# Weight sums on GpSimd one step ahead of their rounding, all in the plain blocks, and attention visits placed by half steps

## Chip, cores and metric

The kernel runs on one core of a Trainium2 chip. The metric is the device time of one execution in microseconds (us). The engines are named as the profile names them: PE (matrix multiply), PEld (its weight loads), DVE (VectorE), ACT (ScalarE), POOL (GpSimd) and SP (SyncE, which here only issues DMAs). Each engine works through its own queue in order; an instruction whose inputs or buffers are not ready holds up everything behind it on that engine.

## What is computed

Local attention over chunks of 64 positions, whose output is the input of a two-layer network with a leaky activation (cut from the reference):

```python
scores = scale * np.matmul(q_c, k_c.transpose(0, 1, 2, 4, 3))   # chunks of 64
scores = scores - np.max(scores, axis=-1, keepdims=True)
attn = np.exp(scores)
attn = attn / (np.sum(attn, axis=-1, keepdims=True) + 1e-09)
out = np.matmul(attn, v_c)                                       # 8 x 8 x 576 x 64
x = out.transpose(0, 2, 1, 3).reshape(4608, 512)
h = x @ w_in                                                     # 512 x 2048
g = np.maximum(h, 0.0) + alpha * np.minimum(h, 0.0)
return g @ w_out                                                 # 2048 x 512
```

## The kernel before

Every float32 product is built from rounded pieces: a value is split into a high part (a rounded copy, by ACT) and a low part (the rest, by DVE), and a product takes three passes on PE.

The 4608 tokens are 36 attention tiles of 128, or nine token blocks of 512. The first three blocks (`PLAIN = 3`) are multiplied plainly, in 48 **steps**; a step is one block with one of 16 slices `f` of the hidden width: `ffn_in` (L318, 12 matmuls into `ps_h`), the activation `prelu` (L308 and L309 on ACT, L310 on DVE), a split (L330 on ACT gives `gh`, L331 on DVE gives `gl`), and `ffn_out` (L343, 12 matmuls into the four accumulators `ps_o0` to `ps_o3`). From step 20 on, the order on PE is kept as written, and the `ffn_out` of a step comes two `ffn_in` later, so the activation has about one step of slack. The steps run over block 0 (3 steps), block 1 (9), block 0 (13), block 1 (7) and block 2 (16). Where a run of steps ends, `store` copies the four accumulators to SBUF (L372, ACT): the first two go into the two halves of one staging buffer named `more`, the others into `ob` and a `g`. The next run of steps cannot write an accumulator before it has been copied.

The other six blocks are taken in three **pairs**, by a scheme with seven instead of eight products of half-size matrices. It needs seven combinations of the quarters of each weight pair. These are made during the plain steps and written to DRAM (`wi_a`, `wo_a`), from where they are streamed back in units of 512 KB. `combine` makes the four combinations that are sums, for one `(side, j)` of 16 (`wi` and `wo`, `j` 0 to 7): it adds high and low parts of two weight tiles back together (L498, two 128x512 adds into buffers `t1`, of which there are two), forms the sums (L505 to L508, four 128x256), rounds them (L519 on ACT, L520 on DVE) into a buffer `raw` (two of them) or `more` (one), and issues four DMAs to DRAM from POOL's queue (L476). `raw` and `more` were the landing buffers of the weights earlier on. A rounding therefore waits until the earlier content of its buffer has been written out, and so does the copy of an accumulator into `more`. The table `COMBINE` names the 14 steps at which a `combine` is emitted; the last two `wo` ones (`LATER`) are made inside the first pair.

`stream` (L540) issues the loads of the combined weights, also on POOL's queue: unit after unit into a ring of four buffers: the two `raw`, and the rooms `wi15` and `wo15` of the last slice's weights, which are free only after the last plain step has used them.

Attention goes on beside all this. For 14 tiles of the plain stage, and for more in the pairs, a **visit** does on PE the value product of an old tile (L279) and the scores of a new one (L201), then the softmax (L217, L218 on DVE, L221 on ACT, L223 to L225 on DVE), a transpose (L232, DVE) and eight small DMAs (L239, SP). The list `visits` names the steps before whose `ffn_in` a visit is placed.

Only PE's order is pinned from step 20 on. The order on the other engines is set by a scheduler that plays the program through in a model of time: what stands late in its model stands late in the queue.

## Time and profile before

| | us |
|---|---|
| median of 3 runs | 849.5 |
| lowest, highest | 849.36, 853.39 |
| the profiled execution | 855.14 |
| its span in the profile | 853.4 |
| PE busy / DVE / ACT / POOL | 810.4 / 672.0 / 544.9 / 208.4 |

The profile is of one execution, which took 5.6 us longer than the median of the others. Its parts used below are: the windows (busy time of each engine in a stretch, then PE's granted clock, the DMA engines' share and GB/s), the waits (who waited for whom: total, times, longest), the timeline (start, duration, engine, line, operation, operands, count, and in brackets the idle time ahead of it with what ended it), the groups by line (count | busy us, mean ns | idle before) and the DMA issues (count, KB each, median us from issue to landing). On this time axis step 20 begins near 158 us, the last plain step's `ffn_out` ends at 349 us, and the first pair's first weight product begins at 350.2 us.

### The profile page before, as it was taken

How to read it: one execution, taken by the hardware profiler on the slowest of the kernel's cores; microseconds unless marked ns; L12 is line 12 of the kernel's file. 1: busy time of each engine (PE TensorE's matmuls, PEld its weight loads, DVE VectorE, ACT ScalarE, POOL GpSimd, SP SyncE). 2: the span in 40 equal slices, each digit the busy share in tenths (PEclk: the TensorE clock that was granted, in tenths of full speed). 3: DMA queues.
4: the chain of work that ended last, by engine and by line, in shares of the span. 5: the costliest groups of instructions: out<-in, count | busy, mean ns of one | idle time of the engine just before them, and what ended most of it. 6: DMA issues, size and time to landing. Idle time of an engine off the chain costs nothing.

```text
span 853.4 us, 15390 instructions
## 1 busy us (share of the span) xinstructions
PE 810.4 (95%) x5248; PEld 645.8 (76%) x5248; DVE 672.0 (79%) x1267; ACT 544.9 (64%) x1392; POOL 208.4 (24%) x331
## 2 busy tenths in 40 slices
PE   4699999999699999999989999999999999999998
PEld 4567788777578778777767878777788778888886
DVE  5788999987978967587869997676689966658875
ACT  5976575656666766677776564777765536556552
POOL 3005223224442230111111233111122321111232
PEclk9899999999899999999999999999999999999999
DMA  9728778548767675679774789776567995555778
GB/s 259 223 72 293 258 234 277 199 150 219 244 173 208 220 247 162 222 255 299 253 259 161 234 230 322 264 246 236 165 203 236 237 310 191 191 180 195 233 222 236
DMA packets 76478, 192.40 MB, mean 225 GB/s; under 512 B 11888, under 2 KB 21104, under 8 KB 76272
## 3 DMA queue, kind: packets, MB, share of 16 engines
q0 software_dynamic: 37600, 125.32, 46.1%
q1 hardware_dynamic: 30656, 51.53, 19.2%
q10 hardware_dynamic: 8144, 14.56, 5.6%
q8 instruction: 42, 0.69, 0.3%
q14 instruction: 36, 0.29, 0.1%
HBM read 135.27 MB, written 42.99 MB: 209 GB/s over the span
## 4 chain that ended last, share of the span: by engine, by line
PE 61%; DMA 13%; DVE 10%; ACT 9%; SPq 4%; issue 2%; POOL 1%; DVEq 0%; ACTq 0%; POOLq 0%
PE ps_o L725 14%; PE ps_h L725 12%; PE ps_o L609 11%; PE ps_o L343 8%; PE ps_h L318 8%; PE ps_h L609 5%; SPq L239 4%; ACT pr L221 3%; DMA pT<-t 3%; DMA v_sb<-v 2%; DMA raw<-w_in 1%; DMA partial<-g 1%; DVE t L232 1%; DMA k_sb<-kT 1%; DMA wi<-qT 1%
## 5 line engine op out<-in xcount | busy, mean ns | idle before, releaser
L343 PE MATMUL ps_o<-wo,gh 128*128 128x512 f32 x384 | 114.6, 395 | 0.0
L318 PE MATMUL ps_h<-xh,wi 128*128 128x512 f32 x384 | 107.0, 402 | 1.1 <-DVE g L310 0.9
L221 ACT ACTIVATE pr<-ps_a,mx 128x64 f32<-128x64 f32 x224 | 67.3, 330 | 30.5 <-DVE mx L218 19.2
L318 PEld LDWEIGHTS ps_h<-xh,wi 128*128 128x128 f32 x384 | 71.5, 190 | 19.2 <-DVE g L310 2.0
L343 PEld LDWEIGHTS ps_o<-wo,gh 128*128 128x128 f32 x384 | 72.0, 188 | 17.4 <-issue 0.3
L609 PE MATMUL ps_o<-wi,raw 128*128 128x512 f32 x225 | 74.6, 399 | 0.7 <-ACT g L630 0.7
L343 PE MATMUL ps_o<-wo,gl 128*128 128x512 f32 x192 | 69.8, 395 | 0.0
L565 ACT CAST gh<-wo 128x512 fp32r<-128x512 f32 x60 | 37.4, 623 | 35.0 <-PE ps_o L725 19.0
L318 PE MATMUL ps_h<-xl,wi 128*128 128x512 f32 x192 | 53.1, 395 | 0.0
L609 PEld LDWEIGHTS ps_o<-wi,raw 128*128 128x128 f32 x225 | 42.0, 188 | 12.1 <-ACT g L630 2.1
L221 ACT ACTIVATION_READ_ACCUMULATOR pr<-ps_a,mx 128x1 f32 x224 | 49.6, 222 | 0.0
L540 POOL DMA_DIRECT2D raw<-wi_a x42 | 22.5, 535 | 107.7 <-PE ps_o L609 61.1
L609 PE MATMUL ps_o<-wo,raw 128*128 128x512 f32 x117 | 46.4, 396 | 0.0
L566 DVE TENSOR_TENSOR gl<-wo,gh 128x512 fp32r<-128x512 f32 x60 | 41.0, 686 | 5.1 <-ACT gh L565 4.8
L609 PE MATMUL ps_o<-wi,wo 128*128 128x512 f32 x126 | 42.9, 398 | 2.1 <-ACT gh L624 1.4
L540 POOL DMA_DIRECT2D raw<-wo_a x42 | 22.4, 535 | 88.9 <-PE ps_o L725 46.8
L330 ACT CAST gh<-g 128x512 fp32r<-128x512 f32 x48 | 29.8, 621 | 22.2 <-DVE g L310 16.6
L343 PEld LDWEIGHTS ps_o<-wo,gl 128*128 128x128 f32 x192 | 36.1, 188 | 8.6
L318 PEld LDWEIGHTS ps_h<-xl,wi 128*128 128x128 f32 x192 | 36.1, 188 | 8.5
L308 ACT ACTIVATE g<-ps_h 128x512 f32<-128x512 f32 x48 | 29.5, 615 | 19.1 <-PE ps_h L318 17.7
L309 ACT ACTIVATE wo<-wo,alpha_sb 128x512 f32<-128x512 f32 x60 | 41.2, 712 | 0.0
L331 DVE TENSOR_TENSOR gl<-g,gh 128x512 fp32r<-128x512 f32 x48 | 32.9, 686 | 7.5 <-ACT gh L330 7.0
(253 smaller groups left out, 2203.3 us busy)
## 6 DMA issues: line engine op xcount, KB each, us to landing
raw<-wi_a POOLq DMA_DIRECT2D x42, 512.0 KB, 4.7
raw<-wo_a POOLq DMA_DIRECT2D x42, 512.0 KB, 4.6
wi<-wi_a POOLq DMA_DIRECT2D x21, 512.0 KB, 4.7
wo<-wi_a POOLq DMA_DIRECT2D x21, 512.0 KB, 5.2
wi<-wo_a POOLq DMA_DIRECT2D x21, 512.0 KB, 4.4
wo<-wo_a POOLq DMA_DIRECT2D x21, 512.0 KB, 4.1
v_sb<-v SPq DMA_DIRECT2D x28, 256.0 KB, 5.2
pT<-t SPq DMA_DIRECT2D x224, 32.0 KB, 3.8
```

The costliest lines, as they stand in the source:

```text
L221: last = nc.scalar.activation(pr[:, g], one, AF.Exp, bias=mx[:, g], scale=SCALE, accum_out=sm[:, g])
L239: nc.sync.dma_start(out=pT[dst, i].rearrange("p h t -> p (h t)"), in_=tb[src, j].rearrange("p h t -> p (h t)"),)
L309: nc.scalar.activation(g, g, AF.Copy, scale=alpha_sb[:, f:f + 1])
L318: pe(nc.tensor.matmul(hps, lhsT=wi[f][:, l, k * P:(k + 1) * P], rhs=xx[:, k], start=(i == 0 and k == 0), stop=(i == 2 and k == NK - 1),))
L330: nc.scalar.copy(gh, g)
L331: low = nc.vector.tensor_tensor(gl, g, f32(gh), op=ALU.subtract)
L343: pe(nc.tensor.matmul(o, lhsT=a[:, ts], rhs=wo[f][:, l], start=(f == first and i == 0), stop=(f == last and i == 2),))
L540: streamed[0] = nc.gpsimd.dma_start(out=f32(t), in_=units[side][n])
L565: hi = nc.scalar.copy(t_hi, t)
L566: return hi, nc.vector.tensor_tensor(t_lo, t, f32(t_hi), op=ALU.subtract)
L609: pe(nc.tensor.matmul(ps, lhsT=w[:, l, k * P:(k + 1) * P], rhs=xx[:, xl], start=first and at == 0, stop=at == n - 1, skip_group_check=not ...
L725: pe(nc.tensor.matmul(ps[m], lhsT=w[:, l, m * P:(m + 1) * P], rhs=xx, start=i != 6 and j == 0 and n == 0, stop=j == JF - 1 and n == 2, ski ...
```

## The change

`combine` is parted. The adds go to GpSimd and fill the two `t1` buffers (`combine`); the rounding and the DMAs are a second function (`round_sums`), which is called at the next step of `COMBINE`, ahead of that step's own sums. `COMBINE` has 17 entries for 16 combinations: all are made in the plain steps, and none in the first pair, where the two `LATER` ones went. With these gone, the list `rooms` (which freed weight buffers later data goes into) becomes a plain one. `visits` is now in half steps: an even number is ahead of that step's `ffn_in` as before, an odd one behind it.

```diff
-    visits = [21, 23, 25, 27, 29, 30, 32, 34, 36, 38, 40, 41, 43, 44]
+    visits = [42, 46, 50, 54, 57, 60, 64, 67, 70, 74, 77, 80, 84, 87]
...
-    def combine(side, j, early, buffers=None):
+    sums_made = []
+
+    def combine(side, j):
...
-            nc.vector.tensor_tensor(t, f32(w[:, 0]), f32(w[:, 1]), op=ALU.add)
+            nc.gpsimd.tensor_tensor(t, f32(w[:, 0]), f32(w[:, 1]), op=ALU.add)
             a.append(t)
...
-        nc.vector.tensor_tensor(a22, a21, a22, op=ALU.add)
-        nc.vector.tensor_tensor(a21, a11, a21, op=ALU.subtract)
-        nc.vector.tensor_tensor(a11, a22, a11, op=ALU.subtract)
-        nc.vector.tensor_tensor(a12, a12, a11, op=ALU.subtract)
+        nc.gpsimd.tensor_tensor(a22, a21, a22, op=ALU.add)
+        nc.gpsimd.tensor_tensor(a21, a11, a21, op=ALU.subtract)
+        nc.gpsimd.tensor_tensor(a11, a22, a11, op=ALU.subtract)
+        nc.gpsimd.tensor_tensor(a12, a12, a11, op=ALU.subtract)
+        sums_made.append((side, j, a))
+
+    def round_sums(early):
+        side, j, a = sums_made.pop()
...
             nc.scalar.copy(w[:, 0], t)
             nc.vector.tensor_tensor(w[:, 1], t, f32(w[:, 0]), op=ALU.subtract)
...
-    COMBINE = (20, 22, 23, 25, 27, 28, 30, 32, 34, 36, 37, 38, 40, 42)
+    COMBINE = (20, 21, 22, 23, 25, 27, 29, 30, 32, 33, 35, 36, 37, 39, 40, 42, 43)
...
-        elif n in COMBINE:
+        if n in COMBINE:
...
-                combine(*combined.pop(0), n in (23, 24, 25, 26, 32, 33, 34))
+                if sums_made:
+                    round_sums(n in (23, 24, 25, 26, 32, 33, 34))
+                if combined:
+                    combine(*combined.pop(0))
...
         pending.append((acc, ffn_in(x[b], f), f, f0, f1, b, False))
+        if 2 * n + 1 in late:
+            visit(*late[2 * n + 1])
...
-            if pair == 0 and j in (2, 4):
-                n = j // 2 - 1
-                with tc.issue_after(stages["softmax"][0].ins), tc.issue_after(stages["softmax"][1].ins):
-                    combine("wo", LATER[n], False, ["more", rooms[14 + 2 * (JF - 3) + n]])
```

Three places show what this does to the queues. In the changed kernel the line numbers are one higher: L520 and L521 are the rounding, L500 and L507 to L510 the sums, L477 the DMAs to DRAM, L541 the unit loads.

**Place one, ACT around the end of block 0 (steps 25 to 27).** Before, the third rounding (the two L519 rows) stood between the accumulators' copies and the next softmax (L221):

```order
L372 COPY ob<-ps_o_1483 128x512
L330 CAST gh<-g 128x512
L372 COPY g<-ps_o_1484 128x512
L372 COPY more<-ps_o_1481 128x512
L372 COPY more<-ps_o_1482 128x512
L519 CAST raw<-t_1972 128x512
L519 CAST raw<-t_1974 128x512
L160 DMA q_sb<-qT 128x512
L162 DMA k_sb<-kT 128x512
L221 ACTIVATE pr,sm<-ps_a,mx 128x64 x8
L304 CAST xh<-ps_a 128x4x64 x2
```

In the changed kernel the third rounding stands a visit and an activation later:

```order
L372 COPY g<-ps_o_1484 128x512
L160 DMA q_sb<-qT 128x512
L162 DMA k_sb<-kT 128x512
L221 ACTIVATE pr,sm<-ps_a,mx 128x64 x8
L304 CAST xh<-ps_a 128x4x64 x2
L308 ACTIVATE g<-ps_h 128x512
L309 ACTIVATE g<-g,alpha_sb 128x512
L330 CAST gh<-g 128x512
L520 CAST raw<-t_1887 128x512
L520 CAST raw<-t_1889 128x512
```

So the two roundings moved behind the softmax, the activation and the `gh` of that step.

**Place two, ACT and POOL around the end of block 1 (steps 31 to 34).** Before, two roundings into `raw` stood a step ahead of the copies into `more` (`ps_o_2336` and `ps_o_2337` are the first two accumulators), and none stood next to them:

```order
L519 CAST raw<-t_2736 128x512
L519 CAST raw<-t_2738 128x512
L309 ACTIVATE g<-g,alpha_sb 128x512
L308 ACTIVATE g<-ps_h 128x512
L330 CAST gh<-g 128x512
L372 COPY more<-ps_o_2336 128x512
L309 ACTIVATE g<-g,alpha_sb 128x512
L372 COPY more<-ps_o_2337 128x512
L372 COPY ob<-ps_o_2338 128x512
L372 COPY g<-ps_o_2339 128x512
```

In the changed kernel (`ps_o_2344` and `ps_o_2345` are the first two accumulators, `ps_o_2347` the last) the copies into `more` stand right behind a rounding that fills the same `more`, and that one behind the activation (L308, L309) of step 34:

```order
L372 COPY g<-ps_o_2347 128x512
L295 COPY xh<-ps_a 128x4x64
L308 ACTIVATE g<-ps_h 128x512
L309 ACTIVATE g<-g,alpha_sb 128x512
L520 CAST raw<-t_2477 128x512
L520 CAST more<-t_2475 128x512
L372 COPY more<-ps_o_2344 128x512
L372 COPY more<-ps_o_2345 128x512
L520 CAST raw<-t_2598 128x512
L520 CAST raw<-t_2600 128x512
L330 CAST gh<-g 128x512
```

On POOL, in the same place, the sums that these roundings read (`t_2475`, `t_2477`), two of the accumulators' DMAs (L377), and the DMAs that empty `raw` and `more`:

```order
L377 DMA partial_2_1423<-ob 128x512
L507 TENSOR_TENSOR t_2477<-t_2477 128x256
L377 DMA partial_3_1427<-g 128x512
L508 TENSOR_TENSOR t_2477<-t_2475,t_2477 128x256
L509 TENSOR_TENSOR t_2475<-t_2477,t_2475 128x256
L510 TENSOR_TENSOR t_2475<-t_2475 128x256
L477 DMA wi_a_379<-raw 128x2x256 x2
L500 TENSOR_TENSOR t_2598<-wi_972 128x512
L477 DMA wi_a_380<-more 128x2x256
L477 DMA wi_a_381<-more 128x2x256
```

Three of the four quarter sums moved behind the DMA of the last accumulator, and a 128x512 add (L500) stands ahead of the two DMAs out of `more`.

**Place three, POOL at the change from the plain steps to the first pair.** Before, the loads of the first two units (`wi_a_358`, `wi_a_359`) stood ahead of those into `wi15` and `wo15` (`wi_3959`, `wo_3997`):

```order
L540 DMA raw<-wi_a_358 128x1024
L476 DMA wo_a_405<-raw 128x2x256
L476 DMA wo_a_393<-raw 128x2x256
L476 DMA wo_a_409<-more 128x2x256
L476 DMA wo_a_401<-more 128x2x256
L540 DMA raw<-wi_a_359 128x1024
L540 DMA wi_3959<-wi_a_360 128x1024
L540 DMA wo_3997<-wi_a_361 128x1024
```

In the changed kernel (`wo_4033` is `wo15`; the first row is the last sum of the last combination):

```order
L510 TENSOR_TENSOR t_3653<-t_3653,t_3651 128x256
L541 DMA wo_4033<-wi_a_361 128x1024
L541 DMA raw<-wi_a_358 128x1024
L477 DMA wo_a_405<-more 128x2x256
L477 DMA wo_a_393<-more 128x2x256
L477 DMA wo_a_409<-raw 128x2x256
L477 DMA wo_a_401<-raw 128x2x256
L541 DMA raw<-wi_a_359 128x1024
```

The first two units that the pair reads (358, then 359) moved behind the fourth (361), and the second of them also behind the last rounding's four DMAs.

More of the change, by code (lines that the diff above doesn't have):

```diff
@@ L472, in unit, with keep_a @@
         return divmod(7 * j + at if side == "wi" else JF * at + j, 2)
-    def keep_a(side, i, j, a, queue=nc.gpsimd):
+    def keep_a(side, i, j, a):
         n, u = unit(side, i, j)
-        queue.dma_start(out=units[side][n][:, u], in_=f32(a))
+        nc.gpsimd.dma_start(out=units[side][n][:, u], in_=f32(a))
     halves = (slice(0, 2 * P), slice(2 * P, 4 * P))
@@ L553, in weight @@
         return ring[0][2][:, u]
[L557 to L562 removed]
+    rooms = [f"{side}{f}" for f in range(NF - 1) for side in ("wi", "wo")]
     def split(t, t_hi, t_lo):
@@ L761, in new_raw @@
             x[b + n] = xp.tile([P, NK, TB], F32, name=name)
[L763 to L764 removed]
+    COMBINE = (20, 21, 22, 23, 25, 27, 29, 30, 32, 33, 35, 36, 37, 39, 40, 42, 43)
+    combined = [(side, j) for side in ("wi", "wo") for j in range(JF)]
     ops, conversion = {}, []
@@ L787, in tile_local_attention_prelu_ffn @@
             attend(st, s)
-        if n in late:
-            if n == visits[0]:
-                attn_load(late[n][1], "q")
-            visit(*late[n])
+        if 2 * n in late:
+            if 2 * n == visits[0]:
+                attn_load(late[2 * n][1], "q")
+            visit(*late[2 * n])
         if ready < NF:
@@ L812, in tile_local_attention_prelu_ffn @@
     conversion.pop(0)()
-    assert not combined and not conversion and not finals
+    assert not combined and not sums_made and not conversion and not finals
     for _ in range(3):
```

25 lines of the change are left out of this document (6 added, 19 removed).

## Prediction

> **What bounds the kernel now.** I read the page's first part, then PE's waits by stretch, then the timeline at the longest wait.
>
> ```profile
> PE 810.4 (95%) x5248; PEld 645.8 (76%) x5248; DVE 672.0 (79%) x1267; ACT 544.9 (64%) x1392; POOL 208.4 (24%) x331
> ```
>
> PE is busy for 95% of the span, so the change can win only where PE waits, and can lose wherever it makes PE wait anew. PE's waits in the plain steps that hold the combinations (195 to 348 us), then in the first pair up to its second product (348 to 456), then in the same stage of the second pair (525 to 626), which has no combinations:
>
> ```profile
> PE ps_a L279 <- issue: 6.5, 1, 6.5
> PE ps_a L279 <- ACT xl L295: 1.1, 1, 1.1
> PE ps_a L279 <- ACT wi L565: 0.7, 1, 0.7
> PE ps_a L201 <- DMA k_sb<-kT: 0.6, 1, 0.6
> ...
> PE ps_o L725 <- DVE gl L566: 3.5, 2, 2.7
> PE ps_o L609 <- ACT gh L624: 1.4, 1, 1.4
> PE ps_h L609 <- ACT gh L624: 1.3, 1, 1.3
> PE ps_o L609 <- ACT g L630: 1.0, 2, 0.7
> PE ps_h L609 <- ACT g L630: 0.3, 1, 0.3
> ...
> PE ps_h L609 <- ACT gh L624: 0.6, 1, 0.6
> PE ps_o L609 <- ACT g L630: 0.3, 1, 0.3
> PE ps_h L609 <- ACT g L630: 0.3, 1, 0.3
> ```
>
> That is 8.9 us in the plain steps, 7.5 in the first pair and 1.2 in the second. The rest of the stage is matmuls end to end, although DVE and ACT are busy there: their load costs nothing as long as nothing blocks them for longer than PE's step of slack. The long wait, on PE and on ACT:
>
> ```profile
> 213.42 0.62 ACT L519 CAST raw<-t 128x512 fp32r<-128x512 f32 x1 [3.41 <-DMA wi_a<-raw]
> 214.72 0.62 ACT L519 CAST raw<-t 128x512 fp32r<-128x512 f32 x1 [0.69 <-DMA wi_a<-raw]
> ...
> 226.03 1.35 PE L279 MATMUL ps_a<-pT,v_sb 64*64 64x64 f32 x29 [6.50 <-issue]
> 229.88 1.10 PE L318 MATMUL ps_h<-xl,wi 128*128 128x512 f32 x4
> ...
> 200.09 0.69 PE L279 MATMUL ps_a<-pT,v_sb 64*64 64x64 f32 x32
> 202.22 1.10 PE L318 MATMUL ps_h<-xl,wi 128*128 128x512 f32 x4
> ```
>
> A rounding on ACT waited 3.41 and 0.69 us for its buffer `raw` to be written out; the softmax and activations behind it came late, and PE stood for 6.5 us. Then it ran slowly: from the visit's start to the second group of L318 it took 3.85 us (226.03 to 229.88), against 2.13 for the same matmuls at 200.09. So the event cost 6.5 + 1.7 = 8.2 us.
>
> **What goes.** (1) At place one of the order the third rounding stands behind the softmax and the activation of the step, and nothing there waits for a write just issued. I drop the 8.2 us. (2) The three short waits of 0.6 to 1.1 us hang on late attention loads and copies, which stay; I count 1 of their 2.3 us. (3) The first pair loses two combinations and their DMAs. It should then wait about as the second pair does: 7.5 - 1.2 = 6.3 at most, and 5 as I take it, since its end also meets the plain blocks' output. Sum: 14.2 us (8.2 to 16.8).
>
> The adds leave DVE: 28 of the first and 56 of the second kind below, 19.2 + 23.7 = 42.9 us in the plain steps. That in itself is worth nothing, since nearly all of it lay beside matmuls.
>
> ```profile
> L498 DVE TENSOR_TENSOR t<-wi 128x512 f32<-128x512 f32 x16 | 10.5, 684 | 0.0
> L507 DVE TENSOR_TENSOR t<-t,t 128x256 f32<-128x256 f32 x16 | 6.8, 423 | 0.3
> ```
>
> The visits on half steps are the same matmuls at 1.1 us (200.09 to 201.19); PE does something else at that moment, so I cost the move at nothing. If it uncovers a late load, that is another wait like the 1.1 above.
>
> **What a sum costs on GpSimd.** No row shows a two-input add there. The nearest POOL rows, and its DMA issues:
>
> ```profile
> L97 POOL MEMSET wi<- 64x512 f32 x4 | 2.1, 519 | 0.2
> masks.py:199 POOL TENSOR_SCALAR_AFFINE_SELECT ident<-ident 128x128 f32<-128x128 f32 x1 | 0.3, 290 | 0.1
> L476 POOL DMA_DIRECT2D wi_a<-raw x24 | 17.5, 730 | 41.5 <-DVE raw L520 41.4
> ```
>
> The memset writes 512 columns in 0.52 us and reads nothing: the low end. The select reads one input: 290 ns for 128 columns, 1.16 us for 512. Twice that, 2.32, is the high end, as there are two inputs. I take 1.16 (the nearest row that reads), and half for 256 columns. A combination is then 2 x 1.16 + 4 x 0.58 + 4 issues x 0.73 = 7.6 us of POOL; 16 of them and 8 us of accumulator DMAs make 130 us, in the 160 us from step 20 to the last rounding. POOL fits, without much room.
>
> Two pages of the Trainium skill bear on this price. "GPSIMD Engine Reference", section 3.1, gives 4497 ns for an add of 2048 columns; by that 512 columns would be an estimated 1.12 us and the sum the same. "SBUF — State Buffer", section "Who interferes with whom", says that a DVE instruction with two SBUF inputs and a GpSimd one that reads SBUF lock each other out for a whole instruction; no run here shows that yet, and it speaks against moving the adds. What it would make of the time is the third case below.
>
> **What comes: the end of block 1 (place two).** Let S be the moment when PE ends the last `ffn_out` of block 1. PE then does one `ffn_in` (2.8 us, 24 matmuls being 5.6 as at 201.19 to 206.88) and at S+2.8 wants the first accumulator, which ACT must have copied into `more`. Before, that copy ran as soon as the accumulator was done, as the timeline shows; in the new order it stands behind a rounding into the same `more`, so it waits until that has been summed, rounded, issued and landed.
>
> ```profile
> 201.19 1.20 PE L318 MATMUL ps_h<-xh,wi 128*128 128x512 f32 x4
> 206.88 1.09 PE L318 MATMUL ps_h<-xh,wi 128*128 128x512 f32 x4
> 250.26 0.40 PE L343 MATMUL ps_o<-wo,gl 128*128 128x512 f32 x1
> 251.00 0.59 ACT L372 COPY more<-ps_o 128x512 f32<-128x512 f32 x1
> ...
> L519 ACT CAST raw<-t 128x512 fp32r<-128x512 f32 x20 | 12.8, 671 | 6.1 <-DMA wi_a<-raw 4.1 <-DVE t L508 2.0
> L377 POOL DMA_DIRECT2D partial<-g x2 | 2.5, 1236 | 0.1
> ...
> wi_a<-more POOLq DMA_DIRECT2D x8, 256.0 KB, 3.8
> ```
>
> The chain: ACT copies the last accumulator at about S+3.4 (an estimate: a visit's softmax, `ob` and `gh` stand ahead of it; sooner is in the low end); POOL issues its DMA (1.24) and does three 256-column sums (1.74): S+6.4. ACT rounds twice (0.6 each): S+7.6. POOL, after the first low part (a DVE add of 0.68 as in L498's row, S+7.7), issues two DMAs out of `raw` (1.46), does the 512-column add (1.16) and starts the second issue out of `more` at S+11.0; it lands 3.8 later, S+14.8; the copy takes 0.6: S+15.4. PE waits 15.4 - 2.8 = **12.6 us**. At the low price the rounding starts when `ffn_in`, L308 and L309 are done, S+4.1, and the same chain gives 9.7; at the high price, with a landing of 4.9, 16.6. The second half of the accumulator copies, the next softmax and `gh` follow within PE's next step.
>
> **What comes: the change to the first pair (place three).** Let X be the end of the last plain `ffn_out` (349.09 before).
>
> ```profile
> 307.65 0.57 POOL L540 DMA_DIRECT2D raw<-wi_a  x1 [4.78 <-issue]
> 315.38 0.57 POOL L540 DMA_DIRECT2D raw<-wi_a  x1 [3.25 <-issue]
> 349.45 0.53 POOL L540 DMA_DIRECT2D wo<-wi_a  x1 [7.17 <-PE ps_o L343]
> 349.09 0.69 PE L279 MATMUL ps_a<-pT,v_sb 64*64 64x64 f32 x32
> 350.18 0.51 PE L609 MATMUL ps_o<-wi,raw 128*128 128x512 f32 x1
> ...
> raw<-wi_a POOLq DMA_DIRECT2D x42, 512.0 KB, 4.7
> wo_a<-raw POOLq DMA_DIRECT2D x16, 256.0 KB, 4.9
> ```
>
> Before, units 358 and 359 were issued at 307.65 and 315.38, some 35 us ahead, and the load into `wo15` waited for PE until 349.45. Now 358 stands behind that load: issued at X+0.9, landed at X+5.6, where PE wants it at X+1.1 (a visit lies between): 4.5 us. Unit 359 stands behind the last rounding, which ACT does only after the third of the four accumulator copies at the end: rounded and read by DVE at X+2.5, issued by X+4.2, landed 4.9 after its start (X+8.4), and only then may 359 be loaded into that `raw`: X+13.2. PE has finished with unit 358 at 5.6 + 2.8 = X+8.4: 4.8 us more. Together **9.3 us** (6 to 12).
>
> **The clock after a wait.** The window over the long wait, and the one over the first pair's 2.7 us wait:
>
> ```profile
> 219.00:229.00 10.00, 3.50 (x69) 2.82 (x68) 9.56 (x23) 6.71 (x25) 3.55 (x5) 0.69 0.63 219
> 440.00:460.00 20.00, 15.85 (x67) 11.94 (x66) 16.98 (x29) 13.98 (x30) 3.08 (x6) 1.00 0.47 171
> ```
>
> A wait of 6.5 us drew the clock down (0.69 in the 10 us), one of 2.7 did not. I add the 1.7 us seen once for place two, and 1.5 for place three, where the two waits lie between those lengths (0 to 3.4).
>
> The Trainium skill ("TensorE: Matmul & The Clock Gate", Part 1) puts the idle time that halves the clock at about 3.4 us; by that both waits of place three would draw it and the sum would be 1.9 us higher. The two rows agree with it.
>
> **The sum.** -14.2 + 12.6 + 9.3 + 3.2 = +10.9 us. Against the profiled execution's own 855.1 that is 866; against the median of 849.5 it is 860.4. The profiled execution is 5.6 us above the median, and I can't see whether the 8.2 us event is as long in the others; if it is shorter there, less is won, so I go a little up: **861 us**.
>
> **The cases.** (a) The forecast, slower by 3 to 20 us: 0.62. For it: both places are fixed by the queues, whatever an add costs; and at place two even the low price leaves 9.7 us. Against it: the landings may be shorter than the medians.
>
> (b) Faster, by one mechanism at place two: the copy into `more` waits only for an older write, not for the rounding just ahead. Then ACT reaches the copy at S+7.6 and the wait is 8.2 - 2.8 = 5.4, without a slow clock; if place three keeps only its first 4.5, the sum is -14.2 + 5.4 + 4.5 = -4.3, 845 us. It decides from a wait at place two under about 6 us. Against it: the rows fill the same single buffer. 0.12.
>
> (c) GpSimd becomes the bound. At the high price a combination takes 4.6 + 4.6 + 2.9 = 12.2 us, 16 make 195, with the accumulators 203 against 160: some 40 us more, about 895. The lock gives nearly the same: six adds that each sit out one 0.69 us DVE instruction make 7.6 + 4.1 = 11.7. It decides from (160 - 8) / 16 = 9.5 us for a combination, 1.65 for a 512-column add. For it: my price is one row scaled by four. 0.13. The page on SBUF named above is the rule behind the second number.
>
> (d) No change: the waits at their low ends (9.7 and 6) and the gain at its high one (16.8): -1 to +3 us. 0.13.
>
> Faster or slower counts from 0.5% (4.2 us), about what a measurement here can tell from no change: faster 0.12, same 0.13, slower 0.75. The range goes from (d) upward into the start of (c): 848 to 880.
>
> **What would show it.** Right: no 6.5 us wait of PE near 219; a PE wait on L343 of 10 us or more where block 2 begins (about 250 us), with the L372 copy into `more` released by a DMA out of `more`; the first L603 waiting for the load of unit 358, and a third matmul group for 359; POOL's 512-column add near 1.2 us; PE's waits in the first pair near 1 to 3 us. Wrong: PE dense through 245 to 265 us (then (b)), or ACT's roundings waiting for POOL all along the plain steps (then (c)).

## The result and the profile after

The changed kernel is slower: 890.62 us median (888.82 to 894.94, 4 runs) against 850.96 (849.36 to 853.39, 4 runs), a ratio of 1.0476 with a 95% interval of 1.0445 to 1.0507. That is 39.7 us in the medians; the two profiled executions lie 33.7 us apart (888.82 and 855.14), and the sums below are made between these two. In the changed kernel `combine`'s sums are L500 and L507 to L510, the rounding L520 and L521, the splits L559 and L560, the unit loads L541, the two weight products L603 and L719.

The page's first part, and the clock in its second, after:

```profile
PE 817.8 (92%) x5248; PEld 649.6 (73%) x5248; DVE 667.8 (75%) x1171; ACT 545.5 (61%) x1392; POOL 310.9 (35%) x435
...
PEclk8999999999968999769999999999999999999999
```

The span grew by 33.6 us (853.4 to 887.0). PE is busy 7.4 us longer for the same 5248 matmuls, which is the slow clock, and idle 26.2 us longer. Its waits in the plain steps (195 to 349 us), then from there into the first pair (349 to 445):

```profile
PE ps_o L343 <- ACT more L372: 18.0, 1, 18.0
PE ps_a L279 <- ACT xl L295: 2.3, 1, 2.3
PE ps_a L279 <- ACT xh L295: 1.5, 1, 1.5
PE ps_a L279 <- issue: 1.3, 1, 1.3
PE ps_a L279 <- DVE xl L305: 0.8, 1, 0.8
PE ps_h L318 <- DVE g L310: 0.4, 1, 0.4
...
PE ps_o L603 <- DMA raw<-wi_a: 10.0, 2, 7.7
PE ps_o L343 <- DVE gl L331: 3.0, 1, 3.0
PE ps_h L318 <- DVE g L310: 2.4, 1, 2.4
PE ps_o L343 <- ACT gh L330: 1.1, 1, 1.1
```

The 6.5 us wait near 219 is gone. Three waits are new: 18.0 us at the start of block 2 (place two), 10.0 at the first two units (place three), and 6.9 in the last plain steps (0.4, 2.4, 1.1 and 3.0; before these were dense), which nobody forecast. The short waits at the visits grew from 2.4 to 5.9 us, and the rest of the first pair fell from 7.5 to 4.7. The sum is 18.0 + 10.0 + 6.9 + 3.5 - 6.5 - 2.8 = 29.1; the start and the later pairs give 2.9 back.

The windows (the last three columns are granted clock, DMA share and GB/s) behind the 18.0, the 2.4, the 3.0 and the 7.7 us waits:

```profile
266.00:276.00 10.00, 8.36 (x86) 6.57 (x87) 3.99 (x6) 2.83 (x5) 7.90 (x11) 0.70 0.55 106
352.00:359.00 7.00, 5.27 (x16) 4.21 (x17) 7.00 (x11) 5.03 (x9) 2.30 (x3) 0.76 0.00 0
368.00:376.00 8.00, 6.11 (x74) 4.56 (x74) 3.96 (x6) 3.38 (x6) 5.82 (x8) 0.60 0.50 184
381.00:391.00 10.00, 5.85 (x14) 4.18 (x15) 0.69 (x1) 0.58 (x1) 1.10 (x2) 0.64 0.70 250
```

Each is a stretch of slow matmuls, and a fifth follows the second wait at the pair (2.4 us; granted clock 0.50 from 391.52 to 394.93). In the five, PE was busy for 22 us at half clock, so these waits cost some 2 us each beyond themselves (an estimate: half of the 22).

**Place two.** Block 1's last `ffn_out` ended at 246.70. The timeline from there, rows of ACT, DVE, POOL and PE:

```profile
249.50 1.31 DVE L218 TENSOR_SCALAR mx<-mx 128x8 f32<-128x8 f32 x1
250.84 0.31 ACT L221 ACTIVATE pr<-ps_a,mx 128x64 f32<-128x64 f32 x1 [2.76 <-DVE mx L218]
...
254.42 0.65 ACT L372 COPY g<-ps_o 128x512 f32<-128x512 f32 x1
...
259.44 0.61 ACT L520 CAST more<-t 128x512 fp32r<-128x512 f32 x1
...
263.38 1.45 POOL L477 DMA_DIRECT2D wi_a<-more  x2
...
267.01 1.07 ACT L372 COPY more<-ps_o 128x512 f32<-128x512 f32 x2 [6.95 <-DMA wi_a<-more]
...
267.64 1.22 PE L343 MATMUL ps_o<-wo,gh 128*128 128x512 f32 x2 [17.98 <-ACT more L372]
```

It is the chain that the prediction drew, 5.4 us longer. Its first link is late: the last accumulator's copy began at 254.42, 7.7 us behind the end of `ffn_out`, where 3.4 had been taken. ACT stood in front of the softmax for 2.76 us, and the DVE instruction that it waited for, 8 columns wide, took 1.31 us.

**DVE.** Its groups in the plain steps (158 to 350 us):

```profile
L331 DVE TENSOR_TENSOR gl<-g,gh 128x512 fp32r<-128x512 f32 x26 | 35.2, 1357 | 13.5 <-ACT gh L330 12.7
L310 DVE SCALAR_TENSOR_TENSOR g<-ps_h,g 128x512 f32<-128x512 f32 x25 | 16.8, 675 | 3.8 <-ACT g L309 3.8
L218 DVE TENSOR_SCALAR mx<-mx 128x8 f32<-128x8 f32 x14 | 11.8, 840 | 0.4
L223 DVE TENSOR_SCALAR sm<-sm 128x8 f32<-128x8 f32 x14 | 7.4, 527 | 29.9 <-ACT pr L221 29.9
```

L331 went from 686 to 1357 ns, L218 from 192 to 840, L223 from 176 to 527, while L310, which reads one input from PSUM, stayed at 675 (680 before). So DVE, though it lost 96 of its 1267 instructions, was held up in others.

**The pace of the combinations.** POOL's timeline over one of them, and the starts of L500 (duration min/median/max, then first and last start):

```profile
284.35 1.45 POOL L477 DMA_DIRECT2D wo_a<-raw  x2 [2.23 <-DVE raw L521]
...
292.34 0.74 POOL L510 TENSOR_TENSOR t<-t,t 128x256 f32<-128x256 f32 x1
296.30 0.73 POOL L477 DMA_DIRECT2D wo_a<-more  x1 [3.21 <-DVE more L521]
...
L500 POOL TENSOR_TENSOR t<-wi x16: 1272/1305/1339, 168.6 to 264.8; 128x512 f32<-128x512 f32 x16
L500 POOL TENSOR_TENSOR t<-wo x16: 1295/1302/5012, 274.5 to 367.0; 128x512 f32<-128x512 f32 x16
```

A 512-column add took 1.30 us and a 256-column one 0.74. POOL works for 8.7 us, then waits 3.2 for the rounding on ACT and DVE, since both `t1` are full: 12.0 us from one combination to the next. Over all 16, the first add of the first began at 168.64 and that of the last at 360.02, 12.8 us from one to the next (367.0 in the rows is the last one's second add), and the last was summed 1.3 us before the plain steps ended (372.28 and 373.56). Before, the eight `wi` ones began 10.2 us apart (171.62 to 243.36). It is POOL that waits in this loop: 44.7 us between 158 and 376 us for the rounding's low parts (L521), while a rounding on ACT waited for POOL's sums once, for 3.2 us.

**Place three**, on POOL and PE:

```profile
373.93 0.57 POOL L541 DMA_DIRECT2D wo<-wi_a  x1 [1.64 <-PE ps_o L343]
374.70 0.56 POOL L541 DMA_DIRECT2D raw<-wi_a  x1 [0.21 <-issue]
...
386.93 0.55 POOL L541 DMA_DIRECT2D raw<-wi_a  x1 [8.39 <-issue]
...
382.75 0.77 PE L603 MATMUL ps_o<-wi,raw 128*128 128x512 f32 x1 [7.65 <-DMA raw<-wi_a]
...
390.61 0.47 PE L603 MATMUL ps_o<-wi,raw 128*128 128x512 f32 x1 [2.39 <-DMA raw<-wi_a]
```

Unit 358 was issued 1.1 us behind the last `ffn_out`, unit 359 only at 386.93, behind the last rounding's DMAs, as the order had shown. But that is 13.4 us behind that end, where 8.4 had been taken: the last of those DMAs was issued by 378.54, and POOL then stood for 8.39 us. The first unit was in use 8.1 us after its issue, where 4.7 had been taken: the load into `wo15` had been issued 0.8 us ahead of it.

### The profile page after: what moved, and what is told of

It is laid out like the page before. It is cut to its first block, busy times and chain, and to the rows that moved or that the text cites. A ratio compares the mean times of both kernels' runs of the same rounds, so it can differ in the third digit from the quotient of the medians.

```text
span 887.0 us, 15397 instructions
## 1 busy us (share of the span) xinstructions
PE 817.8 (92%) x5248; PEld 649.6 (73%) x5248; DVE 667.8 (75%) x1171; ACT 545.5 (61%) x1392; POOL 310.9 (35%) x435
## 4 chain that ended last, share of the span: by engine, by line
PE 49%; DVE 2%; ACT 2%; issue 2%; DMA 2%; DVEq 0%; ACTq 0%; POOLq 0%
PE ps_o L603 16%; PE ps_o L719 14%; PE ps_h L719 11%; PE ps_h L603 7%; PE ps_a L279 1%; DMA k_sb<-kT 1%; DMA v_sb<-v 1%; ACT pr L221 1%; PE ps_a L201 1%; ACT wi L308 0%; ACT wo L308 0%; DMA raw<-wi_a 0%; ACT wo L309 0%; DVE t L232 0%; ACT wi L309 0%
## 5 line engine op out<-in xcount | busy, mean ns | idle before, releaser
L343 PE MATMUL ps_o<-wo,gh 128*128 128x512 f32 x384 | 118.1, 405 | 19.1 <-ACT more L372 18.0
L221 ACT ACTIVATE pr<-ps_a,mx 128x64 f32<-128x64 f32 x224 | 67.1, 325 | 53.9 <-DVE mx L218 43.4
L603 PE MATMUL ps_o<-wi,raw 128*128 128x512 f32 x171 | 70.7, 413 | 10.6 <-DMA raw<-wi_a 10.0
L603 PE MATMUL ps_o<-wo,raw 128*128 128x512 f32 x171 | 70.1, 410 | 0.0
L331 DVE TENSOR_TENSOR gl<-g,gh 128x512 fp32r<-128x512 f32 x48 | 51.3, 1070 | 14.0 <-ACT gh L330 12.7
L541 POOL DMA_DIRECT2D raw<-wi_a x42 | 22.4, 532 | 105.2 <-PE ps_o L603 64.0
L541 POOL DMA_DIRECT2D raw<-wo_a x42 | 22.3, 532 | 92.0 <-PE ps_o L719 48.1
L223 DVE TENSOR_SCALAR sm<-sm 128x8 f32<-128x8 f32 x36 | 11.2, 310 | 54.8 <-ACT pr L221 52.1
L221 ACT ACTIVATION_READ_ACCUMULATOR pr<-ps_a,mx 128x1 f32 x224 | 48.8, 218 | 0.0
L603 PEld LDWEIGHTS ps_o<-wi,raw 128*128 128x128 f32 x171 | 33.4, 195 | 20.4 <-issue 10.8
L308 ACT ACTIVATE wo<-gh 128x512 f32<-128x512 f32 x24 | 15.2, 634 | 52.9 <-DVE gh L626 52.9
L559 ACT CAST gh<-wi 128x512 fp32r<-128x512 f32 x48 | 29.9, 622 | 28.7 <-PE ps_o L719 13.7
L603 PE MATMUL ps_o<-wi,wo 128*128 128x512 f32 x99 | 39.4, 398 | 0.3 <-ACT g L624 0.3
L603 PEld LDWEIGHTS ps_o<-wo,raw 128*128 128x128 f32 x171 | 33.6, 196 | 7.9
```

Source lines behind the costliest of these rows:

```text
L221: last = nc.scalar.activation(pr[:, g], one, AF.Exp, bias=mx[:, g], scale=SCALE, accum_out=sm[:, g])
L223: nc.vector.tensor_scalar(sm, sm, 1e-9, None, op0=ALU.add)
L308: nc.scalar.activation(g, h, AF.Relu, scale=-1.0)
L331: low = nc.vector.tensor_tensor(gl, g, f32(gh), op=ALU.subtract)
L343: pe(nc.tensor.matmul(o, lhsT=a[:, ts], rhs=wo[f][:, l], start=(f == first and i == 0), stop=(f == last and i == 2),))
L541: streamed[0] = nc.gpsimd.dma_start(out=f32(t), in_=units[side][n])
```

## The experiments

The question: is it GpSimd's slowness and its hold on DVE that cost, or the order that the change gives the queues, and why were the sizes wrong? All times are medians, each with the ratio to the kernel before run on the same chip, and its 95% interval.

| kernel | us | ratio (interval) |
|---|---|---|
| the change | 890.6 | 1.0476 (1.0445 to 1.0507) |
| sums on DVE | 847.7 | 0.9954 (0.9934 to 0.9974) |
| round 6 in `raw` | 891.4 | 1.0459 (1.0418 to 1.0500) |
| visits alone | 851.5 | 1.0002 (0.9978 to 1.0025) |
| unread adds beside the kernel before | 871.5 | 1.0224 (1.0192 to 1.0256) |
| unread copies beside it | 865.0 | 1.0158 (1.0112 to 1.0204) |
| two sets of sum buffers | 882.6 | 1.0343 (1.0295 to 1.0390) |
| entries three steps earlier | 883.2 | 1.0366 (1.0313 to 1.0420) |
| the same, more in `raw` | 887.2 | 1.0421 (1.0385 to 1.0456) |
| copies for sums | 883.6 | 1.0356 (1.0313 to 1.0398) |
| 14 on GpSimd | 867.5 | 1.0175 (1.0129 to 1.0222) |
| 14, round 6 in `raw` | 873.6 | 1.0240 (1.0197 to 1.0283) |
| short adds | 912.1 | 1.0695 (1.0653 to 1.0738) |
| sums on DVE, late roundings | 862.0 | 1.0119 (1.0063 to 1.0175) |
| quarter sums on GpSimd | 856.7 | 1.0068 (1.0039 to 1.0097) |
| sums on DVE, third rounding later | 842.7 | 0.9887 (0.9844 to 0.9930) |

### Which part of the change

Sums on DVE:

```diff
-            nc.gpsimd.tensor_tensor(t, f32(w[:, 0]), f32(w[:, 1]), op=ALU.add)
+            nc.vector.tensor_tensor(t, f32(w[:, 0]), f32(w[:, 1]), op=ALU.add)
...
```

> The changed kernel with its six sums per combination back on DVE; all else (16 combinations in the plain steps, rounding one entry later, half-step visits) stays. Theory A (the slow and locking adds of GpSimd, and the late roundings they make, cause the loss): L331 back to about 690 ns and L218 to about 190 ns, the last rounding out before 330 us, units 358 and 359 loaded early, no PE wait over 8 us on L343 at the start of block 2 or on L603; the wait of before at the end of block 0 may come back since the third rounding stands ahead of the softmax again; 845 to 856 us. Theory B (the loss comes from doing all 16 combinations in the plain steps one entry apart and from the moved visits, on whatever engine): PE waits of 10 us or more stay at the start of block 2 and at the first pair; 872 us or more.

847.7 us. DVE's groups, and PE's longest wait in the plain steps:

```profile
L331 DVE TENSOR_TENSOR gl<-g,gh 128x512 fp32r<-128x512 f32 x29 | 19.8, 683 | 1.7 <-ACT gh L330 1.7
...
L218 DVE TENSOR_SCALAR mx<-mx 128x8 f32<-128x8 f32 x15 | 2.5, 167 | 0.1
...
PE ps_a L279 <- issue: 3.2, 1, 3.2
```

Durations are those of before, nothing waits at places two and three, and the whole loss is gone with five engine names. The combinations came 9.9 us apart (first adds from 168.50 to 316.33). Theory B falls. But the scheduler orders the queues anew when the engine changes (unit 358's load moved well ahead of the one into `wo15`), so this alone doesn't part speed from order.

The visits alone, on the kernel before:

```diff
-    visits = [21, 23, 25, 27, 29, 30, 32, 34, 36, 38, 40, 41, 43, 44]
+    visits = [42, 46, 50, 54, 57, 60, 64, 67, 70, 74, 77, 80, 84, 87]
```

> The kernel before with the new list of visits in half steps alone. Theory A: the visits are the same matmuls and cost nothing, 847 to 854 us, PE waits in the plain steps within 3 us of before's 8.9. Rival (the moved visits meet the conversion and the last combinations and make part of the loss): 857 us or more, with new waits of PE between 330 and 350 us.

851.5 us: the visits alone cost nothing that can be measured, as forecast.

### Taking one wait away

Round 6 no longer fills `more` ahead of block 1's store:

```diff
-                    round_sums(n in (23, 24, 25, 26, 32, 33, 34))
+                    round_sums(n in (23, 24, 25, 26, 30, 32, 33, 34))
```

> The changed kernel with one number more in the list of roundings that use only raw (step 30), so that the rounding ahead of block 1's store does not fill more. Theory A, local form (the 18.0 us wait at the start of block 2 is the copy into more waiting for that rounding's DMA, and is worth itself and its slow clock): the wait falls to 0 to 5 us, the rest of the trace stays, 867 to 874 us. Rival (the chain of sums and roundings runs 12 us a combination and sets the end of the plain steps, so a wait taken away early is paid later): the last rounding stays near 372 to 377 us on the axis, PE waits more ahead of the first L603, 882 us or more.

891.4 us: the rival. The 18.0 us wait is gone, and this stands at the pair instead of 10.0:

```profile
PE ps_o L603 <- DMA raw<-wi_a: 25.2, 2, 23.5
```

The chain of combinations ended no sooner (last L500 at 377.2, in the change at 367.0). PE reached the pair sooner and waited there for its end. So the wait at place two was not a cost of its own beside a chain this long: it gave the chain time.

Two fewer combinations in the chain, the last two in the first pair as before:

```diff
-    COMBINE = (20, 21, 22, 23, 25, 27, 29, 30, 32, 33, 35, 36, 37, 39, 40, 42, 43)
+    COMBINE = (20, 21, 22, 23, 25, 27, 29, 30, 32, 33, 35, 36, 37, 39, 40)
```

> The changed kernel with the last two combinations made in the first pair on DVE, as before; 14 on GpSimd in the plain steps. Theory C (16 combinations of 12 us and more are a chain that ends behind the last plain step): the chain ends some 25 us earlier, the waits of 10.0 us for units 358 and 359 and the 6.9 us in the last plain steps go with their slow clock, the 18.0 us at the start of block 2 stays: 866 to 876 us. Rival (waits appear wherever GpSimd and DVE meet, whatever the chain's end): 882 us or more.

867.5 us, as theory C has it: the last 512-column add began at 339.9, units 358 and 359 were loaded from 345.11 and 355.77, PE waited for neither, nor in the last plain steps (0.3 us); the 18.0 at place two stayed. Two combinations are worth 23.1 us, 11.6 each, a little under the pace of the chain.

The same with round 6 in `raw` (the one number of the edit before):

> The run before this one with the rounding of step 30 in raw alone, so that the copy into more waits for no rounding at the start of block 2. Theory C: with the chain shorter the 18.0 us wait there can go without coming back at the end, another 12 to 20 us: 850 to 862 us. Rival (what is won there is lost later, as with 16): within 5 us of the run before this one.

873.6 us, slower than with the wait at place two. Without those 18 us the chain ends late again (last L500 at 351.6), and 7.7 us for the units come back, with waits of 1.4, 1.3 and 3.6 in the plain steps ahead of them. Theory C's bonus was wrong, its mechanism holds.

Three attempts to loosen the chain did little. All entries of `COMBINE` three lower, without and with more roundings in `raw`:

```diff
-    COMBINE = (20, 21, 22, 23, 25, 27, 29, 30, 32, 33, 35, 36, 37, 39, 40, 42, 43)
+    COMBINE = (17, 18, 19, 20, 22, 24, 26, 27, 29, 30, 32, 33, 34, 36, 37, 39, 40)
...
-                    round_sums(n in (23, 24, 25, 26, 32, 33, 34))
+                    round_sums(n in (22, 24, 25, 26, 29, 30, 32, 33, 34))
```

> The changed kernel with all entries of COMBINE three lower, so that the chain of combinations starts some 17 us earlier. Theory C (the chain's length sets the end of the plain steps): the last rounding is issued 10 to 17 us earlier, the wait for unit 358 falls from 7.7 to under 2 us, and those of the last plain steps go; a wait for more at a store stays; 866 to 878 us. Rival D (the waits come from where DVE is held up, not from the chain's end): 884 us or more.

> The run before this one, with the roundings of steps 22, 29 and 30 in raw alone too, so that none ahead of a store fills more. Theory C: with a chain that starts earlier the wait at the start of block 2 can go without being paid at its end; 850 to 862 us, which leaves only what the adds cost DVE. Rival (what is won at one place comes back at another, as it did where only step 30 was changed): within 5 us of the run before this one.

883.2 and 887.2 us. The first sum still began at 168.7 and 169.1, where the weights' own split ends, so the chain did not start earlier and the runs say nothing on theory C. In the first the wait moved to place two (22.6 us) and left the units; in the second it was shared as in the change (17.8 and 10.4), 4 us slower than the first, as the rival had it.

Two sets of sum buffers (7 of 16 combinations in the halves of `more`, all roundings in `raw`):

```diff
-            t = stage.tile([P, 512], F32, name="t1")
+            t = both[:, at] if spare else stage.tile([P, 512], F32, name="t1")
```

> The changed kernel where 7 of the 16 combinations sum into the two halves of more instead of the two buffers t1, so that GpSimd can sum one combination while the one before is still being rounded; all roundings go into raw. Theory C (a serial loop: with two t1 the sums, the rounding and the DMA issues of a combination follow each other, 11 to 13 us each, and 16 of them end only near 377 us): the combinations come 9 to 10 us apart, the last rounding is issued before 345 us on the axis, no PE wait on the load of unit 358, and the time is 858 to 870 us, since what the adds cost DVE stays. Rival D (GpSimd's and DVE's mutual slowing sets the pace, whatever the buffers): the combinations stay 11 us or more apart, the wait on L603 stays, 880 us or more.

882.6 us. The last combination's first add began 19 us earlier (340.6), 6 of them because the first combination did (163.1), and no unit was late, but the copies into `more` at block 1's store then waited for the sums in it (17.2 us), and DVE was held up more (L521 at 1355 ns on average for its `t1` half, 678 in the change). A mixture: the pace went from 12.8 to 11.8 us only, so it shows that the buffers are part of the loop, not what an open one is worth.

### GpSimd's hold on DVE, and its queue

Eight unread adds of 128x256 behind every rounding of the kernel before, whose sums stay on DVE:

```diff
+            nc.gpsimd.tensor_copy(out=idle[:, :8], in_=f32(w[:, 1, :8]))
+            for _ in range(8):
+                nc.gpsimd.tensor_tensor(idle, idle, idle, op=ALU.add)
```

> The kernel before with eight two-input adds of 128x256 on GpSimd behind each combination's rounding in the plain steps; they add up a buffer of their own that nobody reads, so no other engine waits for them by data. Theory A with a lock between GpSimd's adds and DVE: in the plain steps L331 rises from 686 to 900 ns or more and L218 and L223 from under 200 to 300 ns or more, although nothing on DVE needs the adds; the time rises by 3 to 15 us. Rival (DVE in the changed kernel was slow for its own inputs, no lock): L331, L218 and L223 stay within 5 per cent of before's and the time within 3 us.

and twelve copies of 128x128 in their place:

```diff
+            for n in range(12):
+                nc.gpsimd.tensor_copy(out=idle[:, 128 * (n % 2):128 * (n % 2) + 128], in_=idle[:, 128 - 128 * (n % 2):256 - 128 * (n % 2)])
```

> As the run with unread adds on GpSimd beside the kernel before, but with twelve copies of 128x128 (one input) in place of the eight two-input adds of 128x256. Theory: only two-input adds hold DVE up; L331 stays within 5 per cent of 686 ns, L218 and L223 under 210 ns, and the time is within 4 us of before's. Rival: any GpSimd instruction that reads SBUF holds DVE up; L331 at 800 ns or more, L218 at 300 or more, 860 us or more.

871.5 and 865.0 us. L331 and L218 beside the adds, then beside the copies:

```profile
L331 DVE TENSOR_TENSOR gl<-g,gh 128x512 fp32r<-128x512 f32 x27 | 22.4, 828 | 2.9 <-ACT gh L330 2.6
L218 DVE TENSOR_SCALAR mx<-mx 128x8 f32<-128x8 f32 x14 | 5.9, 422 | 0.0
...
L331 DVE TENSOR_TENSOR gl<-g,gh 128x512 fp32r<-128x512 f32 x28 | 19.7, 705 | 8.0 <-ACT gh L330 8.0
L218 DVE TENSOR_SCALAR mx<-mx 128x8 f32<-128x8 f32 x14 | 2.9, 209 | 0.0
```

Nothing on DVE needs the adds, yet it slows down (L331 to 828, short of the 900 expected): the hold is real. The time rose by 20 us, more than the 15 expected. Beside the copies DVE hardly slows, yet 13 us are lost. There PE waited 5.9 us at place two for a copy into `more`, whose DMA stands on POOL's queue among the copies. So work on GpSimd can cost without the hold too, and its queue is the likely way. How the 20 us part is not shown, nor what the hold needs, since these copies are shorter (0.41 us on average) than the adds (0.78).

Copies in the change itself, in place of all its sums. They leave out each sum's second input, so this version times the loop and doesn't compute the function:

```diff
-            nc.gpsimd.tensor_tensor(t, f32(w[:, 0]), f32(w[:, 1]), op=ALU.add)
+            nc.gpsimd.tensor_copy(out=t, in_=f32(w[:, 0]))
...
```

> The changed kernel with each of GpSimd's six sums replaced by a copy of its first input of the same size (the other input, and so the sums of the weight combinations, are left out); order of emission, buffers and DMAs stay. Theory L (the two-input adds hold DVE up, and late DVE work makes the late roundings and the waits): L331 back under 750 ns and L218 under 250 ns; combinations 10 us or less apart; 855 to 868 us. Rival D (the round trip of sums, rounding and DMA issues is too long for any GpSimd instruction of this length): DVE's durations fall but the combinations stay 11 us or more apart and the time is 880 us or more. A third outcome would be that copies of 512 columns hold DVE up as the adds do (L331 at 1000 ns or more); then it tells nothing on the time.

```profile
L500 POOL COPY t<-wi 128x512 f32<-128x512 f32 x16 | 11.2, 699 | 0.0
...
L331 DVE TENSOR_TENSOR gl<-g,gh 128x512 fp32r<-128x512 f32 x28 | 22.6, 808 | 23.7 <-ACT gh L330 22.6 <-PE ps_a L201 0.7
...
PE ps_o L603 <- DMA raw<-wi_a: 21.9, 2, 20.0
```

883.6 us, rival D, with GpSimd's sums nearly halved (3.4 us a combination, 6.3 in the change) and most of the hold gone. The combinations still came 13.2 us apart (first adds from 170.75 to 368.43): POOL now mostly waits 4 to 10 us for a rounding that stands behind a softmax and activations on ACT. The order of ACT's queue is fixed when the program is built, and in it the last three roundings stand behind all 48 activations, as late as in the change or later. So 7 to 10 us of the loss (by the medians, by the ratios) go with GpSimd's speed and hold in such an order; the other 30 stay without them. Late softmaxes don't keep them up either: ACT waited for L218 for 19.5 us here (158 to 373 us), 32.3 in the change and 17.4 before. In the change itself, too, POOL waited for the roundings and not they for POOL. So the order is the likely cause of the 30, but this run doesn't part it from the rest of the loop, since the copies changed the order too.

Every sum cut into pieces of 128 columns:

```diff
+        for at in range(0, to.shape[-1], P):
+            cols = slice(at, at + P)
+            nc.gpsimd.tensor_tensor(to[:, cols], one[:, cols], two[:, cols], op=op)
```

> The changed kernel with every sum on GpSimd cut into pieces of 128 columns, so that one GpSimd instruction is some 0.45 us instead of 1.30 and 0.73. If DVE is held up for one GpSimd instruction at a time (theory L): L218 falls from 840 to 300 to 500 ns, L331 from 1357 to 800 to 1000, while a combination costs GpSimd some 2 us more; if DVE's delay is what costs, the time falls to 870 to 882 us; if GpSimd's own length is what costs (rival D), it rises to 893 us or more.

912.1 us. A piece took 0.50 to 0.57 us on average, and L218 stayed at 837 ns: cutting the instructions did not shorten the hold, and it lengthened the chain (last sum past 400 us). The pieces follow each other without a gap, so the run can't tell a hold by one piece from one by several. It is the slowest version run.

### The order without GpSimd's sums

Sums on DVE, but roundings emitted behind the step's activation and late:

```diff
+    COMBINE = (20, 22, 25, 27, 28, 30, 31, 32, 33, 34, 36, 37, 39, 41, 43, 45, 47)
...
+                    with tc.issue_after(stages["split"][1].ins):
+                        round_sums(n in (23, 24, 25, 26, 32, 33, 34))
```

> All sums on DVE, no arithmetic on GpSimd, but the roundings emitted late (behind the activation of steps 22 to 47), so that the last three stand on ACT behind about as many steps as in the changed kernel (44, 45 and 48 activations ahead of them, there 44, 46 and 48) and unit 359's load stands on GpSimd's queue behind the last rounding's DMAs. Theory Q (the place of the last roundings in the queues costs, whoever adds): PE waits 6 to 12 us for the loads of units 358 and 359, 858 to 868 us. Theory G (only work on GpSimd costs): no such wait, 846 to 853 us.

862.0 us, theory Q, with no arithmetic on GpSimd:

```profile
PE ps_o L603 <- DMA raw<-wi_a: 9.2, 1, 9.2
...
L331 DVE TENSOR_TENSOR gl<-g,gh 128x512 fp32r<-128x512 f32 x29 | 19.8, 682 | 6.8 <-ACT gh L330 6.8
```

So a late order costs at place three whoever adds: 14.3 us over the run with the sums on DVE, for a wait of 9.2, its slow clock and smaller waits. Half of the sums on GpSimd:

```diff
-            nc.gpsimd.tensor_tensor(t, f32(w[:, 0]), f32(w[:, 1]), op=ALU.add)
+            nc.vector.tensor_tensor(t, f32(w[:, 0]), f32(w[:, 1]), op=ALU.add)
```

> The changed kernel with the two 512-column adds of a combination on DVE and the four quarter sums left on GpSimd, which leaves GpSimd 3.0 of its 5.6 us of sums. In its queues the last roundings stand behind 43, 45 and 47 activations instead of 44, 46 and 48. Theory Q (the place in the queues costs): nearly as slow as the changed kernel, 870 us or more, waits at the first pair. Theory G (GpSimd's time and its hold on DVE cost): about half the loss, 860 to 870 us.

856.7 us, faster than either theory gave: 9.0 over all sums on DVE, against 42.9 for all on GpSimd, with one wait of 5.3 us for a unit. The loss is not in proportion to GpSimd's work. Combinations came 10.9 us apart (first adds from 168.33 to 331.46), so the chain's end nearly fits; past that point each further us a combination would count up to 16 times (an estimate, no run shows it).

### A version faster than both

```diff
-    COMBINE = (20, 21, 22, 23, 25, 27, 29, 30, 32, 33, 35, 36, 37, 39, 40, 42, 43)
+    COMBINE = (20, 21, 22, 27, 28, 29, 30, 31, 33, 34, 35, 36, 37, 39, 40, 42, 43)
...
-                    round_sums(n in (23, 24, 25, 26, 32, 33, 34))
+                    round_sums(n in (23, 24, 25, 26, 30, 31, 32, 33, 34))
```

with the sums on DVE.

> The changed kernel with the sums on DVE and COMBINE at 20, 21, 22, 27 to 31, 33 to 37, 39, 40, 42, 43, the roundings of steps 30 and 31 in raw alone: the third rounding then stands behind the softmax that follows block 0's store, and none fills more ahead of block 1's. Expected from the run with the sums on DVE (847.7 us, PE wait of 3.2 and 0.6 us at about 220): that wait goes, 842 to 846 us, faster than both kernels. Rival (the roundings packed closer after step 27 wait for raw's landing and hold the softmax up elsewhere): 847 us or more.

842.7 us (839.0 to 844.5), 1.1% faster than the kernel before. No wait of PE in the plain steps is longer than this, and the granted clock is 0.993 over the span:

```profile
PE ps_a L279 <- issue: 1.7, 1, 1.7
```

All 16 combinations in the plain steps, with the rounding one entry later, are thus a gain once the sums are on DVE: 0.5% as the change had them, 1.1% with the table and two roundings moved. Which part gives how much was not separated.

## Why the prediction went wrong

The sign and the two places were right, the size was not: 39.7 us in the medians, where 10.9 was the sum. The sum had no term for the chain of combinations.

- **The step that failed** is "POOL fits, without much room", under the heading of what a sum costs. The price itself was near: 1.30 and 0.74 us against 1.16 and 0.58, and 2 x 1.30 + 4 x 0.74 + 4 x 0.73 = 8.5 us of POOL instead of 7.6. But it set POOL's busy time (130 us) against 160 us, as if POOL could run ahead. The changed code can't: with two `t1` the next sums wait for the rounding, and the rounding for its place on ACT. What had to be multiplied by 16 is the round trip, 12.8 us on average: some 204 us, from 168.6 to 372.3, where the plain steps ended too (373.56). The order of ACT's queue, there to be read before the run, shows it too: the last roundings stand behind 44, 46 and 48 of 48 activations.
- **Third case.** Its time (895) was nearly met and its threshold for a combination, 9.5 us, was passed, but not by its price: POOL's own 8.5 us lie below it, as does the add's 1.30 below 1.65. Its sign, ACT's roundings waiting for POOL all along the plain steps, did not show: one did, for 3.2 us. So that its time is near is luck. The threshold was too tight as well: 9.9 us, with the sums on DVE, cost nothing, and 10.9, with the quarter sums on GpSimd, a wait of 5.3. Its chance of 0.13 came from asking whether the add is slow, not how long the loop is. That the loss lies mostly in the loop and the order is what the runs with copies, with 14 combinations and with round 6 in `raw` showed.
- **Place two**, 12.6 forecast, 18.0 measured. Releaser and chain were right; the estimate of S+3.4 for the last copy was 4.3 us short, since a softmax that waited for a held DVE instruction stood ahead. Its price as an extra cost was wrong: taking it away alone won nothing.
- **Place three**, 9.3 forecast, 10.0 measured, by the mechanism drawn (7.7 and 2.4 for 4.5 and 4.8). That the totals are close is luck: PE had the second unit 17.1 us behind the last `ffn_out` instead of 13.2, and its work on the first, at a slow clock, filled 5.5 us instead of 2.8. The run with late roundings on DVE has it without GpSimd's sums. The 6.9 us ahead of it were missed: there DVE does the conversion for the pair beside GpSimd's adds.
- **What goes.** The 6.5 us at place one went, as said. The short waits, counted as 1 us less, became 3.5 more, most behind ACT's copies of a visit. The first pair gained 2.8, not 5: the 2.7 us wait where the second product begins stays, with and without the two combinations.
- **Clock.** 1.5 us net forecast, 7.4 measured (PE's busy time): there were five slow stretches, two of them in the last plain steps and two behind waits of 2.4 us, which the reading that one of 2.7 us drew nothing had left out. The length of about 3.4 us that the prediction cites did not decide here either (last section).
- **The lock**, put into the third case as GpSimd waiting for DVE, went mostly the other way. The Trainium skill ("SBUF — State Buffer", section "Who interferes with whom") has both: whichever issues first holds the other up. L331 with two SBUF inputs at 1357 ns agrees, as does one 512-column add of 5.01 us at 360.02, beside DVE's conversion. Its price by itself in the change is not shown; with most of it and half of GpSimd's summing gone, 7 to 10 us were won.
- **Copy waiting only for an older write**: fell; ACT waited 6.95 us for the DMA out of `more`.

Open: how the 20 us of the unread adds part between hold and queue; how the 30 us that stay with copies part between the order and the rest of the loop; and what an open loop with GpSimd's sums would give, since every spare buffer here has another user.

## What to carry to other kernels

When work moves to another engine, price the loop and not the engine: add up one round through every engine until the first buffer comes free, multiply by the rounds, and compare its end with the time of whoever needs the last one. A wait ahead of that end gives the chain time, so mending it alone wins nothing; shorten the chain first. And read the last places in the other queues: an order fixed when the program is built keeps a slow plan even when the engine turns out faster.

## What was not expected of the hardware

Three rows of DVE's and POOL's timeline, one of PE's, and two windows each of the changed kernel and of the one before:

```profile
235.14 2.97 DVE L331 TENSOR_TENSOR gl<-g,gh 128x512 fp32r<-128x512 f32 x1
235.54 1.30 POOL L500 TENSOR_TENSOR t<-wi 128x512 f32<-128x512 f32 x1
236.78 1.45 POOL L477 DMA_DIRECT2D wi_a<-raw  x2
...
353.73 1.89 PE L318 MATMUL ps_h<-xh,wi 128*128 128x512 f32 x4 [2.42 <-DVE g L310]
...
350.56:353.97 3.41, 0.99 (x5) 0.50 (x4) 3.41 (x5) 1.19 (x3) 2.94 (x3) 1.00 0.03 9
353.97:357.38 3.41, 3.41 (x9) 2.65 (x9) 3.41 (x7) 2.76 (x6) 0.00 (x0) 0.50 0.00 0
...
444.59:448.00 3.41, 1.76 (x8) 1.12 (x6) 1.77 (x4) 3.41 (x7) 0.53 (x1) 1.00 0.66 231
448.00:451.41 3.41, 1.66 (x6) 1.05 (x6) 3.41 (x7) 3.00 (x6) 0.00 (x0) 1.00 0.41 144
```

- A DVE instruction that meets GpSimd's adds took four times as long: 2.97 us instead of 0.69. It was held for longer than the add (to 236.84), and ended at 238.11, about when the two DMA issues behind it did (238.23); that these held it is not shown. DMA issues without arithmetic, in the kernel before, left L331 at 686 ns.
- The hold also struck L218, 8 columns wide with one input in SBUF (192 to 840 ns), and did not shrink when GpSimd's adds were cut into pieces (837 ns).
- A single wait of 2.42 us was followed by a group of four matmuls at 1.89 us, 1.10 at full clock; the wait of 2.7 us in the kernel before was not. In both traces the granted clock changes only on a grid of 3.41 us. The first wait lay in one interval of it (350.56 to 353.97, PE busy for 0.99 of 3.41 us, 29%), and the next interval ran at 0.50. The second was cut by a border at 448.00, PE was busy for 52% and 49% of the two intervals, and the clock stayed. Between 60 and 840 us of these two traces, every interval at full clock with PE busy for 44% or less (six of them) was followed by half clock, and none with 49% or more; over all the runs the two kinds overlap between 45% and 54%. So in these traces where a wait lies on the grid counts, not its length alone.
